# Another hand-written order of issue for a linear-attention and token-mixing kernel, with more wide matmul forms and two queues for the first loads

## The chip, the core and the metric

The kernel runs on one core of one Trainium2 chip. The time is device microseconds (us) of one execution. A core has five engines that run side by side and meet at semaphores: TensorE (PE in the profile, its weight loads PEld), VectorE (DVE), ScalarE (ACT), GpSimd (POOL) and SyncE (SP), which here issues transfers. Transfers themselves run on the core's 16 DMA engines.

## What is computed

For 8 batches of 8 heads, with 576 positions and a head size of 64, a linear attention with cosine weights, and then a token mixer over the joined heads:

```python
q_p = phi(q, cos_w, sin_w); k_p = phi(k, cos_w, sin_w)   # relu(x)*cos, relu(x)*sin
kv  = einsum('bhsf,bhsd->bhfd', k_p, v);  z = sum(k_p, axis=2)
num = einsum('bhsf,bhfd->bhsd', q_p, kv)
den = einsum('bhsf,bhf->bhs', q_p, z)[..., None] + 1e-06
x   = (num / den) with heads joined: 8 x 576 x 512
wq, wk = x @ w_q, x @ w_k                                 # 64 wide
mixed  = einsum('bst,btd->bsd', scale * (wq @ wk.T), x)
out    = maximum(mixed, 0) @ w_out                        # 8 x 576 x 512, fp32
```

The kernel never forms wq @ wk.T: it multiplies wk.T with x first.

## The kernel before, in words

**Work units.** A half batch is four heads of one batch (numbers 0 to 15, the H of the code; batch = H // 2). Its q, k and v come as two pieces a and b of 128 x 576 fp32 (0.295 MB each), into four raw buffers per tensor (`NRAW`), which are used in turn: half batch H's load waits until half batch H - 4's values have been read. The position is laid out as 64 partitions x 9, and two heads share the 128 partitions.

**The order.** Nothing is scheduled by a program at run time. `ORDER` (L24) is a string of words; the loop at L588 reads them one by one and emits each word's instructions. Every engine runs its own words in the order in which they stand, and waits by semaphores for what the other engines have to supply; a word that waits holds up all the later words of its engine. A word is a step, a number, `:` a PSUM bank (or pair of banks) and `@` an engine (A ScalarE, V VectorE, G GpSimd).

- **Loads and stores** (`load` L134, `LW` L564, `ST` L561): `LK3b` loads piece b of half batch 3's k, `LW` a weight matrix, `ST5` stores output tile 5 (of 36, each 128 x 512 fp32, 0.262 MB). All stand on SyncE's queue. A store waits for the copy `OE` of the same number, and what stands behind it in the queue waits too.
- **Tables at the start**: `TQ`, `TI`, `TK` on GpSimd (position numbers and an identity), `TV` and `TW` on ScalarE (their sines, with a table load ahead), `TP`, `T2`, `TZ` on VectorE (copies of a table, zeros).
- **Attention of a half batch**: `RK`, `RQ` (L216, L220: relu and cast of k and q), `CV` (L224: cast of v), `VS` (L227: v times cos and sin; on GpSimd two multiplications straight from the raw v, on VectorE one from the cast v). Then TensorE: `QT` or `QU` (transposes of q), `KV` or `KU` (k'v and the row sums of k), and two `N` (numerator and denominator). `QM` (VectorE) multiplies the transposed q with cos and sin on its way out of PSUM, `KE` takes k'v out, `EJ` and `RC` take the denominators and invert them, and two `X` (L340) make x. `XT` or `XR` transposes x, `XE` takes it out.
- **Mixer of a batch**: `WK`, `WQ` (products with the two small weights, `KW` and `QW` take them out), `KX` (wk.T x, taken out by `XK` into two halves of the partitions), `XA` and `XB` (copies of each half across to the other 64 partitions, `copy_across` L514), four `MX` with `ME` (product with wq, relu). Batches 4 and 5 are treated as a pair by another set of words (`WC`, `QC`, `WT`, `KC`, `KP`, `XP`, `MP`, `MM`). For two batches together follow nine `WO` (L547, product with w_out) and `OE` (L555, copy out into one of 16 buffers).

**Two forms of one step.** `KV` (L251) uses 36 matmuls of 64 rows x 64 columns of weights with 130 moving columns, one for each position group, pair of heads and row half; four of them fit on the array beside each other. `KU` (L278) uses 18 of 64 x 128 with 260 moving columns; half of what it computes (products across heads) is not used. `QT` (L263) uses 18 transposes of 64 rows, `QU` (L272) nine of 128 rows; `XR` (L370) 20, `XT` (L359) ten. After `KU`, `KE` takes out a result twice as long, and after `QU`, `QM` is two instructions.

Of the kernel before, what the change touches and what calls it, by code (L numbers as in the profile page):

```python
# [66 lines left out]
def kernel(  # L67
# [66 lines left out]
    def load(nm, H, part):  # L134
        b, h = divmod(H, 2)
        for r in (0, 1) if part is None else (part,):
            nc.sync.dma_start(raw[nm][H % NRAW][:, r, :], src[nm][b][:, 2 * h + r, :])
# [494 lines left out]
```

## Time and profile before

| what | value |
|---|---|
| time, median of 3 runs | 117.86 us (117.85 to 120.2) |
| time of the profiled execution | 117.42 us |
| its span, first to last instruction | 115.4 us |
| mean granted TensorE clock | 0.995 |
| matmuls | 2129 |
| transfers | 39.36 MB, 341 GB/s over the span |
| read, written | 29.62 MB, 9.44 MB |

Engines: PE is matmuls, PEld weight loads, and a busy share is of the span. The slices cut the span into 40 equal parts (2.9 us), with a digit for the busy share of each in tenths. The chain follows the work that ended last back from the last instruction, each piece released by the one ahead of it. In a row of the timeline or of the chain stand start, length, engine, line of the kernel, what it writes and reads, and how many; brackets give the idle time of the engine just before and what ended it. A matmul's row gives its shape as rows * columns of weights, then moving columns. The rows of a group give busy time and mean ns of one. SPq is the queue of SyncE, on which a row is the issue of a transfer, not the transfer.

### The profile page before, as it was taken

The page shows a single profiled execution, that of the slowest core. Times are in us where ns is not written, and L with a number is a line of the kernel's source. Part 1 is how long each engine was busy: PE and PEld are TensorE (multiplying, and loading weights), DVE is VectorE, ACT ScalarE, POOL GpSimd, SP SyncE. Part 2 cuts the span into 40 slices and gives each one's busy share as a digit, 9 for nine tenths or more (in the row PEclk, how much of TensorE's full clock was granted, in tenths as well). Part 3 has the DMA queues.
Part 4 walks back from the last instruction along what each step waited for, and adds up shares of the span by engine and source line. Part 5 has one row for each costly group of instructions (what it writes and reads, how often), then busy time and mean ns, then how long its engine had stood idle before and what let it go on. Part 6 is the DMA issues. An engine that isn't in the chain of part 4 may idle for free.

```text
span 115.4 us, 4951 instructions
## 1 busy us (share of the span) xinstructions
PE 95.5 (83%) x2129; PEld 63.3 (55%) x2129; DVE 83.0 (72%) x138; ACT 73.9 (64%) x124; POOL 72.7 (63%) x64
## 2 busy tenths in 40 slices
PE   0024976648999899999999999999999999999960
...
DMA  3999999999999999999999999999996450199994
GB/s 91 368 379 408 393 392 353 361 385 387 383 363 375 393 385 386 383 398 382 388 384 393 392 394 396 390 397 403 400 407 226 162 190 26 56 349 379 383 383 183
DMA packets 20660, 39.36 MB, mean 341 GB/s; under 512 B 3232, under 2 KB 3232, under 8 KB 20640
## 3 DMA queue, kind: packets, MB, share of 16 engines
...
q8 instruction: 16, 0.26, 0.9%
q14 instruction: 4, 0.03, 0.1%
HBM read 29.62 MB, written 9.44 MB: 339 GB/s over the span
## 4 chain that ended last, share of the span: by engine, by line
PE 64%; DMA 25%; ACT 4%; issue 1%; SPq 1%; POOL 1%; POOLq 0%
PE ps L552 29%; DMA vraw<-in_v_dram 15%; PE ps L319 7%; DMA kraw<-in_k_dram 5%; PE ps L258 5%; DMA qraw<-in_q_dram 5%; PE ps L535 3%; PE ps L276 3%; PE ps L380 2%; PE ps L416 2%; PE ps L403 2%; PE ps L506 2%; PE ps L441 2%; PE ps L367 2%; PE ps L269 1%
## 5 line engine op out<-in xcount | busy, mean ns | idle before, releaser
L233 POOL TENSOR_TENSOR v<-vraw,vtab 128x1152 bf16<-128x1152 f32 x20 | 42.1, 2128 | 3.0 <-PE ps L258 1.2
L552 PE MATMUL ps<-wow,mix 128*128 128x512 bf16 x144 | 34.7, 380 | 0.0
L344 DVE TENSOR_TENSOR x<-ps,rec 128x640 bf16<-128x640 f32 x32 | 24.9, 819 | 0.8
L208 ACT COPY o<-ps 128x512 f32<-128x512 f32 x26 | 15.1, 584 | 8.7 <-PE ps L552 8.7
L552 PEld LDWEIGHTS <-mix 128*128 128x128 bf16 x144 | 12.6, 98 | 14.1 <-issue 1.1
L319 PE MATMUL ps<-kvs,qm 64*128 64x65 bf16 x640 | 13.8, 193 | 1.1 <-ACT kvs L208 1.0
L204 POOL TENSOR_SCALAR rq<-qraw 128x1152 bf16<-128x1152 f32 (+1 forms) x10 | 10.5, 1050 | 6.4 <-DMA qraw<-in_q_dram 6.2
L526 ACT ACTIVATE mix<-ps 128x576 bf16<-128x576 f32 x20 | 12.3, 650 | 3.4 <-PE ps L535 3.0
L319 PEld LDWEIGHTS <-qm 64*128 64x128 bf16 x640 | 12.1, 96 | 3.4 <-issue 1.6
L208 ACT COPY xT<-ps 128x640 f32<-128x640 f32 (+1 forms) x15 | 10.1, 674 | 4.8 <-PE ps L380 2.9
L258 PE MATMUL ps<-v,rk 64*64 64x130 bf16 x468 | 10.6, 234 | 3.1 <-DVE v L236 1.4
L303 DVE TENSOR_TENSOR qm<-ps,qtab 128x2304 bf16<-128x2304 bf16 x9 | 12.2, 1352 | 1.0 <-PE ps L269 1.0
L204 POOL TENSOR_SCALAR rk<-kraw 128x1152 bf16<-128x1152 f32 (+1 forms) x10 | 10.0, 1002 | 4.1 <-DMA kraw<-in_k_dram 3.7
L212 DVE COPY o<-ps 128x512 f32<-128x512 f32 x10 | 6.9, 686 | 7.6 <-PE ps L552 5.2
L258 PEld LDWEIGHTS <-rk 64*64 64x64 bf16 x468 | 8.4, 114 | 5.9 <-issue 2.5
L269 PE MATMUL ps<-ident,rq 64*128 64x64 bf16 x162 | 4.1, 196 | 8.7 <-POOL rq L204 8.4
L208 ACT CAST kvs<-ps 128x260 bf16<-128x260 f32 (+1 forms) x12 | 5.2, 431 | 8.6 <-PE ps L258 7.1
L300 DVE TENSOR_TENSOR qm<-ps,qtab 128x1152 bf16<-128x1152 bf16 x14 | 9.7, 748 | 1.1 <-PE ps L276 1.1
L528 DVE TENSOR_SCALAR mix<-ps 128x576 bf16<-128x576 f32 x12 | 9.0, 753 | 2.1 <-PE ps L486 1.5
L202 ACT ACTIVATE rk<-kraw 128x1152 bf16<-128x1152 f32 (+1 forms) x8 | 8.8, 1103 | 1.6 <-DMA kraw<-in_k_dram 1.6
L236 DVE TENSOR_TENSOR v<-vb,ps 128x1152 bf16<-128x1152 bf16 (+1 forms) x8 | 8.3, 1042 | 1.6 <-POOL vb L210 1.3
L269 PEld LDWEIGHTS <-rq 64*128 64x128 bf16 x162 | 3.2, 98 | 10.0 <-POOL rq L204 9.3
...
## 6 DMA issues: line engine op xcount, KB each, us to landing
kraw<-in_k_dram SPq DMA_DIRECT2D x32, 288.0 KB, 5.9
vraw<-in_v_dram SPq DMA_DIRECT2D x32, 288.0 KB, 5.9
qraw<-in_q_dram SPq DMA_DIRECT2D x32, 288.0 KB, 5.9
...
```

The source lines that it names most:

```text
L202: A.activation(dst, s, AF.Relu)
L204: eng.tensor_scalar(dst, s, FMAX, 0.0, op0=ALU.min, op1=ALU.max)
L208: A.copy(dst, s)
L233: G.tensor_tensor(o[:, :, :, s].rearrange("p r c d -> p (r c) d"), v, vtab[:, 0:n * C, s, 0:1].to_broadcast([P, n * C, D]), op=ALU.mult)
L258: nc.tensor.matmul(kv_v[o, r, :], rk_b[H % NPREP][a, c, pr, :], v2_b[H % NV2][a, pr, c, :, 0:D + 1], start=(c == 0), stop=(c == C - 1))
L300: V.tensor_mul(qm_b[H % NQM][:, s, :, 0:C, :], q, qtab[:, s].unsqueeze(1).to_broadcast([P, 2, C, H2]))
L303: V.tensor_mul(qm_b[H % NQM][:, :, :, 0:C, :].rearrange("p s r c d -> p s r (c d)"), qt_view(at).unsqueeze(1).to_broadcast([P, 2, 2, S]), ...
L319: nc.tensor.matmul(nv[:, pr, u, :], qm_b[H % NQM][a, s, r, 2 * u:2 * u + 2, :], kv_b[H % NKV][a, r, pr if place["KV", H][1] else 0, s, 0:D ...
L344: V.tensor_tensor(x_b[b % NX][:, :, 4 * h:4 * h + 4, :].rearrange("p u (w r) d -> p r w u d", r=2)[:, r], num(place["N", g])[:, :, :, 0:D] ...
L526: A.activation(dst, s, AF.Relu, scale=scale_moe)
L528: V.tensor_scalar(dst, s, scale_moe, 0.0, op0=ALU.mult, op1=ALU.max)
L552: nc.tensor.matmul(o, mix_b[bp % 2][:, m, rt * P:(rt + 1) * P], wow[:, m, :], start=(m == 0), stop=(m == NDM - 1))
```

## The change

The string `ORDER` is replaced by another one. The work is the same; what differs:

- It begins with half batch 0 where the old one began with half batch 1. Three of the first six loads (`LQ0a`, `LV0b`, `LQ0b`) are issued by ScalarE, for which `load` gets an engine; the other loads and all stores stay on SyncE.
- Forms: `KU` for half batches 2, 3, 4, 7, 8, 9, 10, 12 (before 2, 8, 9), `QU` for 1, 2, 4, 5, 6, 7, 9, 10, 15 (before 0, 4, 6, 7, 8, 10, 11), `XT` for 0, 2, 3, 5, 7, 8 (before 1, 2, 5, 6, 9). 2129 matmuls become 2011.
- Engines: whole `VS` go from ten on GpSimd and four on VectorE to eight and six (and four halves on VectorE, as before), whole `CV` from three on GpSimd and one on ScalarE to six on GpSimd; `XE` from 15 on ScalarE and one on VectorE to 11 and five; `KW` all on ScalarE; some `KE`, `QW`, `XK`, `QC`, `KC`, `EJ`, `ME`, `MM`, `RK`, `RQ`, `CW` move singly.
- `copy_across` on ScalarE copies the 256 bf16 values as 128 fp32 words (8 of the 12 copies).
- Stores: `ST11`, `ST7`, `ST1`, `ST0`, `ST9`, `ST13`, `ST17`, `ST6` stand ahead of the last load, which is now `LK15a`; before it was eight others ahead of `LQ14a`.

The diff, with the order cut to the parts spoken of:

```diff
@@ ORDER @@
-TQ TI LK1b LV1a LQ1a TK RQ1a@G LV1b RK1b@G CV1a@A TV TW LQ1b CV1b@A TP0 TZ0@V T2 VS1b@V VS1a@V
-RQ1b@G LK1a QT1:0 RK1a@G LQ0b LQ0a LV0b LV0a LK0b CV0b@G CV0a@G LK0a LV2b LV2a LK2b LK2a QM1
-KV1:2 RQ0b@A KE1@A RQ0a@A LQ2a LQ2b LV3a LV3b LQ3b LW1 LK3b LQ3a RK0a@A LW0 LK3a RK0b@G LV4b LV4a
-VS0b@V LK4a LW2 LQ4b LQ4a CV2@G N3:2 RK2@G LV5a LK4b LQ5a LQ5b LW5 LV5b LW3 RQ2@G LW4 LK5a LK5b
-N2:0 EJ1@V RC1 VS0a@V QU0:4 QM0 KV0:6 KE0@A X3 N0:6 X2 N1:4 VS2@V LV6a LV6b CW1@G CV3@G EJ0@V
-XT1:0 XE1@A RC0 X1 KU2:2 X0 QT2:0 KE2@A XR0:6 XE0@A QM2 RQ3@G VS3@V CW0@G RK3@G WK0:6 N5:0 KW0@A
-KX0:6 XK0@A XB0@A QT3:2 QM3 N4:4 VS4@G KV3:6 EJ2@A RC2 X4 KE3@A XA0@A RK4@G WQ0:2 RQ5@G X5 N6:6
-QW0@A LQ7a LQ6a LQ6b LK6b LK6a LV7b N7:4 MX2:2 ME2@A EJ3@V RC3 CW5@G X7 MX1:0 RQ4@A CV5@G XT2:2
-X6 MX3:4 XR3:6 LV7a LK7b LQ7b LK7a XE2@A XE3@A ME1@V LQ8b QU4:2 QM4 LQ8a ME3@A MX0:0 ME0@A WK1:6
-KV4:4 KW1@V QT5:2 KX1:6 KE4@A LV8b LV8a QM5 WQ1:7 QW1@V N8:4 N9:2 CW2@A CW3@A EJ4@A VS5@V RC4
-XK1@A CW4@G X9 WO3:0 X8 WO1:1 OE1:0@A OE3:1@V RK5@G XB1@G KV5:6 XA1@A MX4:2 KE5@A LV9b LV9a MX6:4
-MX5:6 WO0:1 ME5@A VS6@G ME4@V ME6@V MX7:2 OE0:2@A N11:6 RQ6@A N10:4 ME7@V RK6@A XR4:0 WO5:2 WO2:3
...
-X14 QW2@A X15 XK2@V RK8@A XA2@A XB2@A XR7:4 QT9:0 VS9@V KU8:2 QM9 RQ10@G XE7@A MX8:6 KE8@A WK3:4
-N17:2 KW3@V ME8@A N16:0 EJ8@V RC8 MX11:4 KU9:6 X17 X16 ME11@A WQ3:4 KE9@A QW3@V MX10:2 ME10@A
...
-WC4:4 OE9:14@A XR10:0 LQ15a LV15b ST0 LQ15b LV14b LV14a ST8 LK12a LK12b X23 LK14a LK14b LV15a
-ST13 ST16 ST3 LK15b LK15a ST7 LQ14a ST5 ST12 ST15 RQ12@G VS12@G X22 XR11:6 QC4@V XE10@A QT13:2
...
-WO29:0 MX30:4 ME30@A WO30:1 WO31:4 OE30:13@A OE29:7@V WO33:5 OE31:8@A WO34:4 ST10 ST23 WO35:1
-ST21 ST19 ST22 ST1 ST26 ST25 ST18 OE33:3@A ST27 ST28 ST9 ST20 WO32:5 ST30 OE34:10@A ST31 ST29
-ST33 OE32:2@A ST34 OE35:1@V ST35 ST32
+LK0b LQ0a@A LV0a LV0b@A LK0a LQ0b@A TQ TI RQ0a@G TK TV RK0b@A TW CV0b@A CV0a@A RK0a@A LQ1a
+RQ0b@A LV1a LQ1b LV1b LK1a TP0 T2 LK1b LV2a LV2b LK2b LQ2b LQ2a LK2a LQ3b LQ3a LW0 LW1 LV3a LV3b
+RQ1b@G CV1b@G CV1a@A RQ1a@A VS0b@V LK3a LK3b LV4a VS0a@V LV4b LK4b LK4a TZ0@V QT0:0 KV0:2 KE0@A
+LQ4a QM0 LQ4b VS1a@V LQ5b LQ5a VS1b@V LW3 QU1:4 LW4 LV5a LV5b LW5 RK1a@G LW2 RK1b@A LK5b LK5a
+N1:2 VS2@G LV6b LV6a N0:0 EJ0@A QM1 RC0 X1 KV1:6 KE1@A N3:6 N2:4 RQ2@A CW1@G CW0@G CV3@G X0
+RK2@A RQ3@A EJ1@V XT0:0 RC1 X2 QU2:4 X3 XR1:6 KU2:2 QM2 QT3:4 KE2@A N4:2 XE0@A XE1@V N5:6 WK0:0
+QM3 EJ2@V RC2 VS3@V RK3@G KW0@A WQ0:4 KX0:5 XK0@A QW0@A XB0@A X5 KU3:0 CV4@G RK4@G KE3@A X4
+MX2:6 RQ4@G VS4@V MX3:4 RQ5@G XT2:2 N6:0 ME3@A N7:4 CV5@G CW5@G LQ7a LQ6a ME2@A RK5@G EJ3@V
+XE2@A XA0@A LQ6b LK6b LK6a LQ7b RC3 X7 KU4:6 MX0:2 ME0@A QU4:4 X6 XT3:0 KE4@A MX1:6 QU5:2 QM4
+XE3@A WK1:0 ME1@V QM5 CW4@A N8:4 KW1@A CW3@A CW2@A N9:6 KX1:0 WQ1:1 EJ4@V RC4 LQ8a X8 LV7a LV7b
+LK7b LK7a WO3:2 LV8a LV8b X9 VS5@V WO2:3 LQ8b LV9a LK8b LK8a LV9b VS6@G RQ6@G QW1@A OE3:0@A
+XK1@A XB1@A OE2:1@V WO0:2 OE0:2@V XA1@A MX7:0 RQ7@G MX4:6 ME4@A KV5:4 KE5@A MX6:2 ME6@V ME7@A
+LQ11a LK9b LQ9b LQ9a LV10b LK9a LV10a CV7@G WO1:6 OE1:3@A MX5:0 ME5@V N10:2 N11:4 EJ5@A RK7@G
...
+OE4:8@A ME10@V LK11b QT8:6 RK8@A XR6:2 XE6@V KU7:4 MX9:0 QM8 KE7@A ME9@A KU8:2 KE8@A N15:4 MX8:0
+ME8@A MX11:6 ME11@V VS9@G N14:2 RQ9@A EJ7@V WO11:6 OE11:9@A RC7 RK9@A WO12:0 X15 X14 LV13a LQ11b
+LQ12a LV13b QU9:6 N17:2 N16:4 OE12:10@V EJ8@A KU9:0 QM9 VS10@G KE9@A RC8 X17 XT7:6 N19:0 X16
+N18:2 EJ9@V RC9 XE7@A WK3:6 X19 X18 RK10@A KW3@A WQ3:4 CV11@G KX3:5 KU10:0 QW3@A RQ10@G VS11@V
...
+WO9:5 XP2@A QM12 MP19:2 MP21:6 MM19@V MP18:0 OE9:9@A MM21@V MM18@A WO16:4 MP16:0 MP23:2 KU12:6
+OE16:7@A KE12@A MM16@A MM23@V ST9 CV14@G RQ14@G MP22:2 KV13:4 LK15b ST13 ST17 ST6 LK15a ST2 ST5
...
+WO32:6 WO31:4 WO34:5 OE30:3@A OE29:2@V WO35:1 OE32:9@V OE34:14@V ST14 ST16 ST25 ST20 OE31:6@A
+WO33:0 ST8 ST3 ST19 ST30 ST29 OE35:12@A ST32 ST27 ST31 ST34 ST35 OE33:8@V ST33 WO28:1 OE28:15@A
+ST28
@@ -131,10 +132,10 @@
 
     src = {"k": srcs(k), "q": srcs(q), "v": srcs(v)}
 
-    def load(nm, H, part):
+    def load(nm, H, part, eng):
         b, h = divmod(H, 2)
         for r in (0, 1) if part is None else (part,):
-            nc.sync.dma_start(raw[nm][H % NRAW][:, r, :], src[nm][b][:, 2 * h + r, :])
+            (eng or nc.sync).dma_start(raw[nm][H % NRAW][:, r, :], src[nm][b][:, 2 * h + r, :])
 
     coef = math.pi / 2.0 / S
     ki = pool.tile([P, C, 2], I32, name="ki")
@@ -512,8 +513,11 @@
         cast(eng, kx_b[b % 2][:, 0, :], bank(place["KX", b])[:, 0:XC])
 
     def copy_across(b, t, eng):
-        cast(eng, kx_b[b % 2][H2 * (1 - t):H2 * (2 - t), 1, :],
-             kx_b[b % 2][H2 * t:H2 * t + H2, 0, :])
+        dst = kx_b[b % 2][H2 * (1 - t):H2 * (2 - t), 1, :]
+        s = kx_b[b % 2][H2 * t:H2 * t + H2, 0, :]
+        if eng is A:
+            dst, s = dst.bitcast(FP32), s.bitcast(FP32)
+        cast(eng, dst, s)
 
     def XA(b, ps, eng):
         copy_across(b, 0, eng)
@@ -593,7 +597,7 @@
         kind = word[:2] if word[:2] in steps or word[0] in "LRCVT" else word[0]
         i, ps = int(word[len(kind):] or 0), int(ps or 0)
         if kind in ("LK", "LQ", "LV"):
-            load(kind[1].lower(), i, part)
+            load(kind[1].lower(), i, part, ENG.get(eng))
         elif kind in halves:
             halves[kind](i, ps, ENG.get(eng), slice(0, 2) if part is None else
                          slice(part, part + 1))
```

More of the change, by code (lines that the diff above doesn't have):

```diff
@@ L49 @@
-ST13 ST16 ST3 LK15b LK15a ST7 LQ14a ST5 ST12 ST15 RQ12@G VS12@G X22 XR11:6 QC4@V XE10@A QT13:2
-WO14:4 ST11 XE11@V WC5:6 WO17:5 QM13 QC5@V QT12:2 WT2:6 KC2@V RK13@A VS13@G RK12@G OE14:15@A QM12
-OE17:8@A RQ15@A WO10:4 KP2:5 OE10:3@A KV13:2 XP2@A MP22:4 KE13@A MP20:6 MM22@A MM20@V MP16:0
-MM16@A KV12:2 MP23:4 KE12@V MP21:6 MM21@V MM23@A MP19:0 MM19@A N25:2 N24:4 MP18:6 MM18@A EJ12@V
-RC12 WO21:0 X25 WO26:1 X24 MP17:2 N27:6 OE21:2@A OE26:6@A N26:4 QT15:0 EJ13@A MM17@V WO25:2
-WO24:3 RC13 RK15@A RQ14@A X27 X26 OE24:13@A OE25:12@A VS15@G WO19:6 QM15 KV15:4 KE15@A ST14
@@ L55 @@
-XR13:2 OE19:1@V ST24 ST6 ST17 QT14:0 XE13@A N31:4 N30:6 RK14@G VS14@G EJ15@A WO18:2 WO22:3 QM14
-RC15 OE18:5@A X30 X31 OE22:4@A KV14:0 XR12:6 XR15:4 KE14@V XE12@A N29:0 N28:2 EJ14@V WK6:6 RC14
-X29 WQ6:7 KW6@A X28 QW6@A KX6:6 XE15@A XK6@A XA6@G WO23:0 XR14:6 MX24:4 OE23:10@V ME24@V XE14@A
-XB6@A WO20:2 WK7:3 MX25:4 MX27:6 KW7@V OE20:11@A ME27@A ME25@V MX26:0 WQ7:2 ME26@A KX7:3 WO28:0
-WO27:1 OE27:9@V XK7@A XA7@A QW7@A XB7@G MX28:2 MX29:4 MX31:6 OE28:15@A ME29@A ME28@V ME31@A
-WO29:0 MX30:4 ME30@A WO30:1 WO31:4 OE30:13@A OE29:7@V WO33:5 OE31:8@A WO34:4 ST10 ST23 WO35:1
@@ new lines @@
+LV15a ST0 LV14a LQ15b LQ15a KV11:2 LK14b QM10 QT11:0 ME15@A MX14:6 KE11@A N20:4 VS13@G RQ12@G
+N21:2 VS12@G QM11 ME14@A RK13@G RK12@G EJ10@V WO17:6 RC10 WO10:0 OE17:11@A X20 OE10:12@A N22:6
+X21 N23:4 EJ11@V RC11 X22 XR9:2 WO14:0 OE14:13@A XE9@A WO13:1 XR10:6 XE10@A RQ13@A X23 XR11:4
+OE13:14@V WC4:2 XE11@V WC5:4 WO15:6 QC4@V QC5@A WT2:4 QT13:2 QT12:0 OE15:15@A KC2@A KP2:4 QM13
+WO9:5 XP2@A QM12 MP19:2 MP21:6 MM19@V MP18:0 OE9:9@A MM21@V MM18@A WO16:4 MP16:0 MP23:2 KU12:6
+OE16:7@A KE12@A MM16@A MM23@V ST9 CV14@G RQ14@G MP22:2 KV13:4 LK15b ST13 ST17 ST6 LK15a ST2 ST5
```

22 lines of the change are left out of this document (13 added, 9 removed).

## The prediction, before any run

> **What bounds the kernel now.** I read the page's busy table and slices first, then the chain, then the timeline of the first 36 us, then the groups by line.
>
> ```profile
> PE 95.5 (83%) x2129; PEld 63.3 (55%) x2129; DVE 83.0 (72%) x138; ACT 73.9 (64%) x124; POOL 72.7 (63%) x64
> PE   0024976648999899999999999999999999999960
> DMA  3999999999999999999999999999996450199994
> GB/s 91 368 379 408 393 392 353 361 385 387 383 363 375 393 385 386 383 398 382 388 384 393 392 394 396 390 397 403 400 407 226 162 190 26 56 349 379 383 383 183
> ```
>
> A slice is 2.9 us. The DMA engines are full from slice 2 to slice 30, at about 0.38 MB per us; TensorE has holes until slice 11 and none after it. So there are two stages. Up to about 33 us the arrival of the inputs sets the pace. From there TensorE does, and the transfers have slack: they fall to 26 GB/s while TensorE stays full, and rise again when the last stores come. The chain says the same in time:
>
> ```profile
> 25.60 5.88 DMA qraw<-in_q_dram
> 31.65 1.16 POOL rq L204
> 32.85 0.44 PE ps L269 x18
> 37.24 0.49 issue
> 39.20 0.97 PE ps L552 x4
> 41.31 1.83 PE ps L552 x8
> 48.88 0.72 PE ps L258 x35
> 58.35 1.01 PE ps L284 x18
> 70.06 0.65 PE ps L258 x35
> 87.57 2.72 PE ps L552 x12
> 111.63 0.58 ACT o L208
> ```
>
> The columns are start, length and what. A transfer of q for half batch 5 lands, GpSimd does its relu (RQ5), the transposes QT5 follow, and then TensorE's steps run one after another until 111.6 us; after that come one output copy and one store. The first output step, WO3, is the mark between the two stages in both orders: in both it follows WQ1, and the steps ahead of it are the same work.
>
> ```profile
> 35.16 1.90 PE L552 MATMUL ps<-wow,mix 128*128 128x512 bf16 x8
> ```
>
> From WO3 to TensorE's end are 111.6 - 35.2 = 76.4 us. The profiled execution took 117.42 us with a span of 115.4, so 2.0 us lie around the span; the median of the runs is 117.86. The sum below is made against 117.42.
>
> **Part 1: the wide forms, after WO3.** Only forms change; every half batch still gets its steps. Eight KU for three and eight KV for thirteen take 90 matmuls out, nine QU for seven another 18, six XT for five 10: 2129 - 118 = 2011. What a form costs TensorE is read from the chain. Four WO matmuls with another shape behind them took 0.97 us, eight took 1.83, twelve 2.72: a WO takes 0.87, and a change of the matmul shape (128*128, 64*128, 64*64, 128*64) 0.1. KV took 0.65 with one such change behind it, so 0.56 by itself; KU (18 matmuls, 260 columns, two at a time) took 1.01. A KU in place of a KV thus costs 0.46 us and can save shape changes, because N, MX, XR and QT have its shape 64*128. Behind WO3 the new order has three more KU (7, 10, 12), as many QU and XT as before, and I count 54 shape changes against 59. 3 x 0.46 - 5 x 0.1 = **+0.9 us**, on the path, with nothing to hide it. Bounds: +0.4 (if the changes of shape saved are worth twice that) to +1.4 (if nothing).
>
> **Part 2: the start.** The new order begins with half batch 0 and waits more on ScalarE.
>
> ```profile
> 3.05 0.43 SPq L137 DMA_DIRECT2D kraw<-in_k_dram  x1
> 4.32 0.67 ACT L208 CAST vb<-vraw 128x576 bf16<-128x576 f32 x1 [2.30 <-DMA vraw<-in_v_dram]
> 6.47 1.15 ACT L182 ACTIVATE qtab<-wof 128x1152 bf16<-128x1152 int32 x1
> 7.81 0.66 PE L269 MATMUL ps<-ident,rq 64*128 64x64 bf16 x18 [7.81 <-POOL rq L204]
> 8.50 0.68 ACT L202 ACTIVATE rq<-qraw 128x576 bf16<-128x576 f32 x1 [0.33 <-DMA qraw<-in_q_dram]
> L167 ACT ACT_TABLE_LOAD x1 | 1.3, 1283 | 0.0
> qraw<-in_q_dram SPq DMA_DIRECT2D x32, 288.0 KB, 5.9
> ```
>
> The sixth transfer is issued at 3.05 us already, one per 0.47 us, while 0.295 MB need 0.78 us at 0.38 MB per us: issue is ahead of the data. Two queues therefore bring the six transfers at most the 0.4 us of one issue; I take 0. ScalarE now issues three of them (3 x 0.43) before its table load (1.28), which is free, since TV waits for TK, and TK now stands behind RQ0a on GpSimd: RQ0a starts with its data at about 4.3 (as the cast of v did), 0.67, TK 0.5, so TV at 5.5 and RK0b at 5.7. Then in ScalarE's order TW 1.1, two casts of v, RK0a and RQ0b at 0.67 each: RQ0b ends at about 10.0. QT0, which needs it, starts at 10.05 against 7.81 now: **2.2 us late**. KV0, KE0 and N0 wait behind it in turn. What hides this is the pace of the data:
>
> ```profile
> 24.50 1.15 POOL L204 TENSOR_SCALAR rk<-kraw 128x1152 bf16<-128x1152 f32 x1
> 25.70 0.72 PE L258 MATMUL ps<-v,rk 64*64 64x130 bf16 x36 [1.17 <-POOL rk L204]
> 30.09 1.15 POOL L204 TENSOR_SCALAR rk<-kraw 128x1152 bf16<-128x1152 f32 x1
> 31.65 1.15 POOL L204 TENSOR_SCALAR rq<-qraw 128x1152 bf16<-128x1152 f32 x1 [0.41 <-DMA qraw<-in_q_dram]
> ```
>
> Half batch 3's k is complete after 7.34 MB of loads in both orders, so RK3 again ends at 25.6 and KU3 starts there. Adding up TensorE's steps ahead of it (KV1 13.9, XT0 16.8, KU2 19.1, WK0 21.7, KX0 22.9) I find it ready at 23.6: the late start is used up with 2 us to spare, and KX0 and WQ0 lie ahead of KU3. Half batch 5's q is complete at 9.70 MB, now at 10.26, 0.56 / 0.38 = 1.5 us earlier: RQ5 runs from 30.15 to 31.3. Meanwhile VectorE, which has VS3 and VS4 now (1.27 each; VS4 was GpSimd's), goes VS3 25.4, X5, X4 26.9, VS4 28.2, EJ3, RC3, X7, X6 30.2; so KU4 28.2 to 29.3, QU4 29.7, XT3 30.3, QU5 31.3, and back to back WK1 0.68, N8 and N9 0.7, KX1 0.65, WQ1 0.6: WO3 at 34.55, **-0.6 us**. KU3's, KU4's, QU1's and QU2's greater length lies in these waits for data; without that cover it is 2 x 0.46 and 2 x 0.25. Bounds: -1.0 (the two queues bring their 0.4) to +2.2 (the late start is not absorbed).
>
> **Part 3: the other engines.** Busy times now, and what moves:
>
> ```profile
> L233 POOL TENSOR_TENSOR v<-vraw,vtab 128x1152 bf16<-128x1152 f32 x20 | 42.1, 2128 | 3.0 <-PE ps L258 1.2 <-DVE x L344 1.0 <-DMA vraw<-in_v_dram 0.7
> L236 DVE TENSOR_TENSOR v<-vb,ps 128x2304 bf16<-128x2304 bf16 x4 | 5.4, 1346 | 1.3 <-POOL vb L210 1.3
> L210 POOL TENSOR_SCALAR vb<-vraw 128x1152 bf16<-128x1152 f32 x3 | 3.5, 1151 | 1.7 <-DMA vraw<-in_v_dram 1.7
> L208 ACT COPY xT<-ps 128x640 f32<-128x640 f32 x10 | 6.9, 692 | 2.9 <-PE ps L380 2.9
> L212 DVE COPY xT<-ps 128x1280 bf16<-128x1280 bf16 x1 | 0.8, 811 | 0.0
> L208 ACT COPY kx<-kx 64x256 bf16<-64x256 bf16 x9 | 3.6, 403 | 0.2
> 35.00:60.00 25.00, 24.06 (x538) 16.48 (x530) 22.98 (x39) 17.83 (x29) 20.77 (x14) 1.00 1.04 387
> ```
>
> GpSimd loses two VS (2 x 4.26) and gets three casts of v (3 x 1.15), with small moves some 6 us less. VectorE gets two VS (2.7) and four XE (3.2), and gives three KW, a KE, an XK, a QW, a QC and a KC (2.9): some +3 us. ScalarE gives the XE and one table load; eight copies across halves as 128 fp32 words instead of 256 bf16 save something like 0.1 each: some 1.4 us less. None of this is on TensorE's path unless TensorE comes to wait. It does already a little: From WO3 on, 36 WO at 0.86, 9 KV 0.56, 22 N 0.31, 28 MX and MP 0.12, 9 XR 0.29, 5 QU 0.50, 5 QT 0.26, 3 XT 0.56, 2 KU 1.02, 4 each of WK, WQ and KX 0.59, 0.50 and 0.56, 2 WC 0.98, KP and WT 1.2 make 65.9 us (the shortest of each kind in the chain), and 59 shape changes 5.6: so 4.9 us of the 76.4 are small stops, such as the 0.49 in KV5, which waits for nothing that the profile shows. VectorE is the one to watch: 22.98 busy of 25 us from 35 to 60. For stops I take 0.1 less for the shorter copies, with bounds of -2.5 (half of them go) and +2.6 (VectorE sets the pace, below).
>
> **Part 4: stores.** Eight stores stand ahead of the last load in both orders, so this load lands at about the same time; ST9 asks for OE9, which I place at 79 us, about 1.6 us after its turn, behind which LK15b waits, but eight transfers in flight (5.9 us) cover that. Behind the last load the queue stood still in the old order; the new one has more stores that are ready:
>
> ```profile
> 81.60 30.97 SPq L562 DMA_DIRECT2D out_dram<-o  x28
> 95.00:100.00 5.00, 5.00 (x135) 3.40 (x128) 3.22 (x7) 3.00 (x6) 0.40 (x1) 1.00 0.09 32
> ```
>
> The last store is issued right after its copy now, so an earlier drain brings nothing: 0.
>
> **The sum:** 117.42 - 0.6 + 0.9 - 0.1 = **117.6 us**, 0.3 below the median shown: no change that 2% (2.4 us, about what a measurement of this kernel can tell from no change) would show.
>
> **The rivals.**
> (B) The small stops go. GpSimd's relief and the other order take half of the 4.9 us out, and the two queues bring their 0.4: 117.42 - 1.0 + 0.9 - 2.5 = 114.8. For it: ScalarE and GpSimd have less to do. Against: each stop is short, and VectorE has more.
> (C) Slower, the late start is carried: if TensorE isn't ready at 23.6 but later than 25.6, every further us is paid at WO3. With the whole 2.2: 117.42 + 2.2 + 0.9 = 120.5. For it: five ScalarE steps in a row stand ahead of QT0. Against: the 2 us to spare.
> (D) VectorE becomes the bound behind WO3. From RC4 to RC14, whose rows are
>
> ```profile
> 36.23 0.27 DVE L338 RECIPROCAL rec<-rec 128x20 f32<-128x20 f32 x1
> 96.36 0.28 DVE L338 RECIPROCAL rec<-rec 128x20 f32<-128x20 f32 x1
> ```
>
> it has 52.3 us of work by the groups' means against 50.1 now, done in 60.1 us; at the same ratio 62.7, +2.6: 117.42 - 0.6 + 2.6 = 119.4, part 1 hidden behind it.
> (E) What counts is the number of matmuls. By the page's 95.5 us for 2129, 118 fewer are worth 5.3 us: 112.1. Against: KV's 36 took 0.65, KU's 18 took 1.01.
> [...]
> (F) The two queues and the fp32 copies do nothing and ST9's stop does reach the last k (KV15): 1.6 more, 119.2.
>
> **How the numbers follow.** Forecast 0.50 (its own range 116.2 to 119.0), B 0.22, C 0.13, D 0.09, E 0.03, F 0.03. Faster by over 2% (under 115.5): most of B, E, a little of the forecast's edge, 0.24. Slower (over 120.2): most of C, a third of D, 0.14. Within: 0.62. The range 114.5 to 120.8 goes a little past B's value and C's, and leaves out the outer parts of B and C, and E.
>
> **What would show it.** Right: QT0 at about 10 us; KU3 at 25 to 26 and released by RK3; WO3 at 34 to 35; KU 1.0 us each with KV at 0.65; 77 us from WO3 to the last matmul; no transfers waiting at the end. Wrong: WO3 later than 36 (C), VectorE over 94% busy in a stretch of 20 us while TensorE has holes (D), WO3 to the end under 75 us (B).

## The result, and the profile after

| | before | after |
|---|---|---|
| median of 20 runs each, us | 118.12 (116.81 to 120.2) | 119.25 (118.32 to 120.47) |
| ratio, with its 95% interval | | 1.0117 [1.0084, 1.0151] |
| span of the profiled execution, us | 115.4 | 116.9 |

The change makes the kernel slower by 1.2%, some 1.4 us (the medians differ by 1.1); the forecast was 0.15% above the profiled time of before and 0.3 us below the median shown with it, that is, no change. Ratios here leave out runs more than 1.5% above a kernel's fastest one, so they can differ from the ratio of the medians (most in experiment 4). One kernel varies by 1 to 2 us either way from run to run. The profiled execution of before (117.42 us) lies below its kernel's median, that of after (119.83 us) above, so this pair lies further apart than usual.

The page of the changed kernel: span, busy times, three rows of slices (2.92 us each) and the two queues over which the engines' own instructions come (packets, MB, share).

```profile
span 116.9 us, 4706 instructions
...
PE 96.0 (82%) x1997; PEld 65.0 (56%) x2011; DVE 86.8 (74%) x139; ACT 71.9 (62%) x127; POOL 66.8 (57%) x61
...
PE   0004977967999899998999979999998999999940
...
DMA  3999999999999999999999999995993198980992
GB/s 87 393 399 389 393 384 336 393 390 389 385 393 392 391 387 386 391 390 396 387 391 395 403 394 397 368 390 208 296 373 147 53 379 331 344 333 8 353 377 81
...
q8 instruction: 15, 0.25, 0.9%
q14 instruction: 5, 0.04, 0.1%
```

The two stages are still there: transfers full to slice 27, then TensorE. (14 matmul records are missing in this trace; 2011 weight loads are there.) Behind slice 11 TensorE has an 8, a 7 and an 8 (slices 19, 24 and 31) where before had nines. New is the 8 GB/s of slice 37 (105 to 108 us), where the stores stand, and the last two queue rows, which matter below.

The timeline's rows of the marks (start, length, matmuls of QT0, KU3, WO3), then pieces of the chain (start, length, what):

```profile
10.26 0.67 PE L270 MATMUL ps<-ident,rq 64*128 64x64 bf16 x18 [10.26 <-ACT rq L203]
...
24.94 1.19 PE L285 MATMUL ps<-v,rk 64*128 64x260 bf16 x18 [0.91 <-POOL rk L205]
...
34.44 1.89 PE L556 MATMUL ps<-wow,mix 128*128 128x512 bf16 x7
```

```profile
51.21 1.01 PE ps L285 x18
...
69.41 0.61 issue
70.02 0.38 PE ps L556
...
106.18 6.16 PE ps L556 x28
...
112.36 0.59 ACT o L209
```

The start came as forecast, and so did KU's 1.01 us. TensorE ends at 112.34 (106.18 + 6.16), 0.7 us later than before although it reached WO3 0.7 us earlier. The account, profile against profile; "stops" are all gaps over 0.09 us behind WO3 in which TensorE neither multiplies nor loads weights, from the trace's records; "work" is the rest:

| | before | after | difference | forecast |
|---|---|---|---|---|
| to WO3 | 35.16 | 34.44 | -0.7 | -0.6 |
| WO3 to last matmul, work | 75.45 | 76.24 | +0.8 | +0.9 |
| the same, stops | 0.99 | 1.66 | +0.7 | -0.1 |
| last store's issue to its last packet | 1.76 | 2.45 | +0.7 | 0 |

The row of the stops is the least certain. 0.12 of the 1.66 us, ahead of WO9, is a matmul without a record: the traces of experiments 3 and 13, which have all of them, show no gap there. And stops differ between executions of one order: the traces of experiments 9 and 14, in which TensorE's instructions are those of before, have 2.7 and 1.9 us of them.

**The end.** The transfers from 110 us to the end of the span, before and then after, 0.14 and 0.17 us to a number:

```profile
DMA  9999999999998999999999999989700000000000
GB/s 364 394 394 349 395 379 425 349 380 349 394 440 334 410 349 394 349 379 455 349 394 334 394 380 379 440 334 410 258 0 0 0 0 0 0 0 0 0 0 0
...
q1 hardware_dynamic: 818, 1.48, 73.3%
```

```profile
GB/s 392 380 356 404 392 416 297 416 427 380 356 380 416 380 368 392 380 368 392 380 356 356 345 356 416 356 60 12 24 24 36 0 0 0 0 0 0 0 0 0
...
q1 hardware_dynamic: 951, 1.72, 66.5%
q14 instruction: 1, 0.01, 0.5%
```

Before, all transfers stop together. After, a rest goes on at some 24 GB/s: by the records, 8 packets of the last store (2 KB, 84 ns each) run one behind the other from 114.78 to 115.43, alone. 8 are one engine's share of a store's 128 packets, and 24 GB/s about a sixteenth of the 385 or so ahead of them, so 15 engines have stopped and one goes on (the records don't name it). And in this window, and not in that of before, there is one packet of the instruction queue q14, 8 KB, from 114.23 to 114.78: the 8 packets begin when it ends.

**A stop in the middle.** The 0.61 us of "issue" stand ahead of the last of WO10's four matmuls. A window on the transfers just ahead of it:

```profile
q1 hardware_dynamic: 223, 0.45, 99.5%
q8 instruction: 1, 0.02, 5.6%
```

Among the loads runs one packet of the other instruction queue, 16 KB, by the records from 67.56 to 68.64; TensorE goes on at 70.02, 1.39 us after its end. This gave a theory: **TensorE runs out of instructions.** The trace of before has 16 such packets for 4258 matmuls and weight loads, that of after 15 for 4022: 266 and 268 to a packet. I took a packet for a block of 256 instructions; that length is shown by the places of the stops, below. Its rival was that the order lost time to waits for data of VectorE, ScalarE and GpSimd.

### The profile page after: what moved, and what is told of

It reads as the page before. It is cut to its first block, busy times and chain, and to the rows that moved or that the text cites. A ratio compares the mean times of both kernels' runs of the same rounds, so it can differ in the third digit from the quotient of the medians.

```text
span 116.9 us, 4706 instructions
## 1 busy us (share of the span) xinstructions
PE 96.0 (82%) x1997; PEld 65.0 (56%) x2011; DVE 86.8 (74%) x139; ACT 71.9 (62%) x127; POOL 66.8 (57%) x61
## 4 chain that ended last, share of the span: by engine, by line
PE 57%; DMA 20%; DVE 11%; ACT 4%; issue 2%; POOL 1%; ACTq 0%; SPq 0%; POOLq 0%; DVEq 0%
PE ps L556 23%; DMA vraw<-in_v_dram 9%; DMA qraw<-in_q_dram 6%; PE ps L285 6%; PE ps L320 5%; DMA kraw<-in_k_dram 5%; DVE v L237 3%; PE ps L539 3%; PE ps L277 3%; DVE x L345 3%; PE ps L381 3%; PE ps L404 2%; PE ps L259 2%; PE ps L507 2%; PE ps L417 2%
## 5 line engine op out<-in xcount | busy, mean ns | idle before, releaser
L234 POOL TENSOR_TENSOR v<-vraw,vtab 128x1152 bf16<-128x1152 f32 x16 | 33.7, 2129 | 5.8 <-PE ps L320 1.8
L301 DVE TENSOR_TENSOR qm<-ps,qtab 128x1152 bf16<-128x1152 bf16 x18 | 12.7, 749 | 1.0 <-ACT o L209 0.5
L237 DVE TENSOR_TENSOR v<-vb,ps 128x2304 bf16<-128x2304 bf16 (+1 forms) x10 | 10.9, 1110 | 3.1 <-ACT vb L209 1.8
L532 DVE TENSOR_SCALAR mix<-ps 128x576 bf16<-128x576 f32 x14 | 10.5, 753 | 3.7 <-PE ps L539 2.8
L304 DVE TENSOR_TENSOR qm<-ps,qtab 128x2304 bf16<-128x2304 bf16 x7 | 9.4, 1352 | 2.2 <-PE ps L270 1.9
L285 PE MATMUL ps<-v,rk 64*128 64x260 bf16 x144 | 9.6, 271 | 1.6 <-POOL rk L205 0.9
L211 POOL TENSOR_SCALAR vb<-vraw 128x1152 bf16<-128x1152 f32 (+1 forms) x7 | 7.6, 1083 | 4.8 <-DMA vraw<-in_v_dram 4.7
L209 ACT CAST kvs<-ps 128x520 bf16<-128x520 f32 (+1 forms) x13 | 6.4, 494 | 5.7 <-PE ps L285 3.0
L211 POOL TENSOR_SCALAR kx<-kx 64x256 bf16<-64x256 bf16 x4 | 1.6, 399 | 14.0 <-ACT kx L209 13.8
L285 PEld LDWEIGHTS <-rk 64*128 64x128 bf16 x144 | 7.1, 93 | 3.0 <-POOL rk L205 1.4
```

The costliest lines, as they stand in the source:

```text
L209: A.copy(dst, s)
L234: G.tensor_tensor(o[:, :, :, s].rearrange("p r c d -> p (r c) d"), v, vtab[:, 0:n * C, s, 0:1].to_broadcast([P, n * C, D]), op=ALU.mult)
L237: V.tensor_mul(o.rearrange("p r c s (h e) -> p (r c) s h e", e=2), vb_b[H % NPREP][:, part].rearrange("p r c (h e) -> p (r c) h e", e=2).u ...
L285: nc.tensor.matmul(o[:, r, :], rk_b[H % NPREP][a, c, :, :], v2_b[H % NV2][a, :, c, :, 0:D + 1], start=(c == 0), stop=(c == C - 1))
L301: V.tensor_mul(qm_b[H % NQM][:, s, :, 0:C, :], q, qtab[:, s].unsqueeze(1).to_broadcast([P, 2, C, H2]))
L532: V.tensor_scalar(dst, s, scale_moe, 0.0, op0=ALU.mult, op1=ALU.max)
```

## The experiments

All were timed in 5 rounds against the kernel before on the same chip: 1 to 4, 5 to 12, 13 to 15 and 16 to 18 on one chip each. What the change does is undone in parts first (1 to 4), then the instruction blocks are shifted (5 to 7, 10, 11), then the end is tested (8, 9, 13, 16 to 18); 12 and 14 put parts of the change into the kernel before, and 15 joins the two orders once more. "Theory" and "rival" are those of the text recorded for each experiment.

**1 and 2, the two halves of the order.** The new order up to WO3 with the old one behind it, and the reverse; steps already done are left out of the second part.

```diff
 # 1: new order ... LV7b LK7b LK7a
-WO3:2 LV8a LV8b X9 ...
+LQ8b LV8b LV8a QW1@V VS5@V XK1@A X9 WO3:0 WO1:1 ... (old order to its end)
```

> The new order's words up to WO3, then the old order's words (less those already done), so the new start with the old middle and end. My account of the 1.4 us: the start gains 0.7 at WO3 (34.45 against 35.16 in the profiles) and the rest loses about 2.2. By it this kernel is 0.7 us faster than before, ratio 0.994, WO3 at 34.5. Rival (what the start gains is given back later, because data or stores set the end anyway): ratio 1.000 within 0.003. Second rival (the late first transposes are what costs): 1.005 or more.

Measured 119.41 us, 1.0136 [1.0081, 1.0190]. WO3 came at 34.45, yet the last matmul at 113.43: stops of 0.84 (KV5), 0.85 (N15), 0.71 (XR11) and 0.42 us (N29) took the gain and more; work from WO3 on was 75.40, as before. By its size this is the second rival, but not by its reason, as WO3 came as early as expected.

> The old order's words up to WO3, then the new order's. By my account 2.2 us slower than before, ratio 1.018, WO3 at 35.2. Rival (the start is given back): 1.012, as the changed kernel. Second rival (the start costs): 1.005 or less.

Measured 123.69 us, 1.0454 [1.0387, 1.0522], far above both. A stop of 2.26 us ahead of WO3 itself (released by VectorE's X), and two of 0.57 and 0.59 us. Right behind the first one the granted clock was 0.5 from 38.05 to 41.47 us, and twelve WO matmuls took 4.45 us there, against 2.72 in the kernel before: 1.7 us of the time is the clock. So neither half has a price of its own: what is done ahead decides where the other half stops.

**3, the stores.** ST27, ready first, ahead of ST30, for which the queue stood.

```diff
-ST30 ST29 OE35:12@A ST32 ST27
+ST27 ST30 ST29 OE35:12@A ST32
```

> The new order with one word moved: ST27 stands ahead of ST30 in SyncE's queue instead of behind ST30, ST29 and ST32. In the new profile OE27 is ready at 105.3 and ST27 is issued at 109.2, behind ST30, which waits for OE30 until 107.4, while the DMA engines move 80 GB/s. My account: the ten stores from 107.4 on are more than the engines can move until the last copy (113.0), and the last store lands 0.75 us later after its issue than it did before; with nine it is 0.6 to 0.7 us faster than the new order, ratio to before 1.006. Rival (TensorE and the last copy set the end, the longer last landing is chance): as the new order, 1.012.

Measured 119.06 us, 1.0098 [1.0056, 1.0140], an interval that holds both values; the trace decides for the rival. The late engine was there again, behind a q14 packet from 114.13 to 114.88, and last issue to last packet was 2.41 us.

**4, the three wide forms undone.**

```diff
-KU7:4 ... KU10:0 ... KU12:6
+KV7:4 ... KV10:0 ... KV12:6
```

> The new order with KV in place of KU for half batches 7, 10 and 12, nothing else. My sum: three times 0.46 us of streaming back, five changes of matmul shape more: 0.9 us faster than the new order, ratio to before 1.004, TensorE's last matmul at 111.4 instead of 112.3. Rival (TensorE's added streaming lies in waits for the other engines): as the new order, 1.012.

Measured 121.86 us, 1.0151 [1.0084, 1.0219] for the faster of its runs (two of six): not cheaper, as my sum had it; whether dearer than the change (1.0117), these two don't say. The chain of its profiled execution (123.06 us) has

```profile
67.83 2.34 issue
...
100.42 0.47 issue
```

and a stop of 0.95 us at KV10. A KV is 72 instructions where KU is 36. Right behind the stop of 2.34 us the granted clock was 0.5 again, from 69.94 to 73.36, so the work from WO3 on, 77.1 us, doesn't price the forms. Without the 1.7 us that the clock cost in experiment 2 it is 75.4 (an estimate), 0.8 less than after, about what part 1 has for the forms.

**5, 6, 7: the blocks shifted.** One-column matmuls of a zeroed tile, two instructions each, run in the first 3 us, where TensorE has nothing to do. They move every later instruction by 224, 256 (one whole block) and 280 places.

```diff
     def WU(i, ps, eng):
-        pass
+        V.memset(zt, 0.0)
+        for j in range(i):
+            a, o = (slice(H2 * r, H2 * r + H2) for r in (j % 2, j // 2 % 2))
+            nc.tensor.matmul(bank(ps + j % 2)[o, 0:1], zt[a, 0:H2], zt[a, H2:H2 + 1],
+                             start=True, stop=True)
 # ORDER begins with WU112:4, WU128:4 or WU140:4
```

> The changed kernel with 112 one-column matmuls of a zeroed tile on TensorE ahead of everything, where TensorE stands idle; they write a PSUM bank that is overwritten later. Each is two instructions, so every later instruction of TensorE stands 224 places further on in the blocks of 256 in which its instructions are fetched. Theory (TensorE's program is fetched too slowly where many small matmuls stand close): at this shift the shortest time between a block's start and the place 70 instructions ahead of its end is 4.3 us, against 3.35 us without it (at 69 us, where the 0.61 us stop stands), so that stop goes and no new one comes: ratio to before about 1.006, 0.6 us less than the change. Rival (the 0.61 us stop is a wait for data or a property of that matmul): the stop stays at the same matmul, ratio 1.012.

> The same with 128 matmuls, 256 instructions: one whole block, so every place within a block is as in the change. Both theories: ratio about 1.012, the 0.61 us stop ahead of the same matmul. If the idle matmuls by themselves changed the time (TensorE's clock at the start), it would show here.

> The same with 140 matmuls, 280 instructions: 24 places beyond one block. Theory: the shortest stretch is now 1.8 to 2.3 us (at 67 us, ahead of N20 to N23), while a fetch needs some 3.6 us to be usable; a stop of about 1.6 us there instead of 0.61, so 1 us more than the change: ratio about 1.021. Rival (stop not from the fetch): 1.012, the same stop of 0.61 us.

Measured 1.0120 [1.0085, 1.0155], 1.0072 [1.0041, 1.0102] and 1.0217 [1.0158, 1.0276]. With 140 the stop is now 1.18 us at N21, with another of 0.77 at KU10 (its chain has both),

```profile
63.64 0.77 issue
...
68.88 1.18 issue
```

and the kernel is 1.7 us slower than with 128 (120.87 against 119.18): the theory. With 128 a stop stands ahead of the same matmul of WO10 as forecast, but of 0.27 us, and one of 0.35 us stands one block earlier. With 112 the stop at WO10 is gone as expected, but no time was gained: in all three a wait for data of 0.4 us at WO5 came in (13, 16 and 17, without idle matmuls, have it too) and WO3 was 0.1 to 0.3 us later. The expectation of 1.006 failed.

The proof is the place of the stops. The next fences give for several kernels the time up to a stop with TensorE's busy time and the number of its matmuls and weight loads so far (first two groups); the first fence is the kernel before (its 0.49 us at KV5), then experiments 9 (0.25, 0.86, 0.76 us), 10 (1.20 us) and 12 (0.60, 1.26 us).

```profile
0.00:37.30 37.30, 22.25 (x606) 17.33 (x607) 25.85 (x46) 18.64 (x33) 25.04 (x36) 1.00 1.00 357
```

```profile
0.00:36.95 36.95, 22.21 (x606) 17.33 (x607) 26.17 (x47) 19.22 (x39) 24.99 (x36) 1.00 1.00 359
0.00:54.90 54.90, 39.36 (x990) 28.93 (x990) 42.18 (x75) 32.23 (x58) 40.06 (x44) 1.00 1.02 369
0.00:60.65 60.65, 44.25 (x1118) 32.97 (x1118) 47.12 (x82) 36.56 (x65) 45.27 (x48) 1.00 1.02 371
```

```profile
0.00:62.90 62.90, 48.19 (x1246) 35.76 (x1246) 47.89 (x83) 36.73 (x61) 46.84 (x49) 0.95 1.02 369
```

```profile
0.00:55.65 55.65, 40.77 (x990) 30.18 (x990) 42.82 (x75) 32.39 (x53) 40.07 (x44) 1.00 1.01 365
0.00:75.10 75.10, 59.31 (x1374) 43.16 (x1374) 58.71 (x102) 47.48 (x77) 56.31 (x54) 1.00 1.01 366
```

Add the two: 1213, 1980, 2236, 2492 and 2748. They lie 256 apart (1213 is 1212 and one), whatever the step is called: 606 + 607 in two kernels, 990 + 990 in two. In all, 30 stops of 0.2 us and more in 15 of the 20 traces stand within three instructions of such a place, and 29 of them ended 1.26 to 1.54 us after a 16 KB packet of q8 had ended (experiment 12's second at 76.33, its packet at 75.02; experiment 10's at 64.03, its packet at 62.64). The thirtieth, 0.44 us at N11 in experiment 15, is a wait for data. Counted on from 1212 in steps of 256, 16 such places lie in the kernel before (188 to 4028) and 15 in the changed one, as many as the packets of each. In the kernel before the packets began 2.3 to 3.8 us after TensorE had passed one of these places as long as the transfers were full (13 packets) and 0.7 to 1.6 us after it later, ended ahead of the next place, and took 0.9 to 1.1 us among full loads. That a packet begins only then is not shown: in the trace of after, the first twelve began 1.8 to 4.0 us after their places, the thirteenth 0.7 us ahead of its own, and the last two 1.3 and 0.5 us behind theirs. 3.0 + 1.05 + 1.4 makes 5.5 us a block (an estimate from the times of the kernel before and the 1.26 to 1.54 us). In experiment 9, TensorE went on at 55.72 and stood again at 60.61: 256 instructions in 4.9 us, and then 0.76 us without.

**10 and 11, shifts chosen to avoid the stops.** 84 idle matmuls ahead of the kernel before, 12 ahead of experiment 1's.

> The kernel before with 84 idle one-column matmuls (168 instructions) ahead of everything on TensorE. Theory of the fetch: at this shift no stretch between 30 and 92 us is shorter than 3.6 us (2.7 and 2.8 us at 84 and 72 us without it), so the stop of 0.49 us ahead of KV5 goes; with the 0.4 us that the idle matmuls cost the changed kernel by themselves elsewhere, ratio 0.996 to 1.000. Rival (KV5 waits for its data): the stop of 0.49 us stays at KV5, ratio 1.000 to 1.004.

> The first experiment again (the new order up to WO3, the old one behind it; ratio 1.0136, with stops of 0.84, 0.85, 0.71 and 0.42 us) with 12 idle matmuls, 24 instructions, ahead of everything on TensorE. Theory of the fetch: at this shift the shortest stretches behind WO3 are 3.3 us and more (2.65 us at 51 us without it); the stops at KV5, N15 and XR11 shrink from 2.4 us in sum to 0.5 to 1 us and the ratio to 0.998 to 1.003. Rival (the start's gain is lost to waits for data of VectorE and ScalarE): the stops stay at the same matmuls, ratio 1.0136.

Measured 1.0136 [1.0075, 1.0198] and 1.0078 [1.0034, 1.0122]; both expectations failed in size. In 10 the stop at KV5 went, but one of 1.20 us came at N18, and the profiled execution had a granted clock of 0.5 from 23.7 to 30.5 us and WO3 at 37.2; why the clock fell is open. In 11 the stops at N15, XR11 and N29 went as expected; the 0.76 us at KV5 stayed, so that one is a wait for data (it isn't at a block's end either). In 10 a stretch that I had called safe held a stop, because I had reckoned a fetch, and the 3.6 us that the expectation of 7 gives it (my estimate), from the wrong place: a block is entered some 60 counted instructions earlier than I took it, at the places above.

**12, the wide forms alone.** KV7, KV10 and KV12 of the kernel before made KU.

> The kernel before with KV7, KV10 and KV12 in the wide form and nothing else of the change. By the sum of the prediction (three times 0.46 less the shape changes 0.1 to 0.3): TensorE streams 1.0 to 1.3 us longer between WO3 and its last matmul, 76.5 us instead of 75.45 once the stops are taken off; ratio 1.009 if the stops stay as they are. Theory of the fetch: the three save 36 instructions each, so the stops move; between 0.5 us less and 1 us more of them. Rival (the wide form is no dearer among other work): streaming 75.5 us, ratio 1.000.

Measured 120.50 us, 1.0224 [1.0177, 1.0271]. Work from WO3 on was 75.92, only 0.47 more than before: the forms themselves cost half of what I expected, perhaps since a KU next to N, MX or XR saves more shape changes. But the stops were 3.01 us, 0.60 and 1.26 of it at block ends (0.99, 1.9 and 2.7 in the traces of before, 14 and 9), and the last store was late too. Three forms that cost half a microsecond cost 2.6 in this order.

**8, one queue for the first six transfers.**

```diff
-LK0b LQ0a@A LV0a LV0b@A LK0a LQ0b@A
+LK0b LQ0a LV0a LV0b LK0a LQ0b
```

> The changed kernel with the first six transfers all on SP's queue, so that ScalarE issues three instructions less. Theory of the tail (a fetch of 8 KB of ScalarE's own instructions, started 1.9 us after its instruction 190 or 191, occupies one DMA engine at 114.2 to 114.8 and makes the last store's share of that engine 0.7 us late): with 188 instructions ahead of the end it starts only after the last store, span less last issue goes from 3.9 to 3.1 us, and the ratio to 1.005 if the start is not later; if QT0 moves from 10.26 to 10.6 the gain is less by as much. Rival (the late engine has another cause): the tail stays 3.9 us, ratio 1.011 to 1.014.

Measured 119.19 us, 1.0080 [1.0026, 1.0134], between the two. The end is the theory's: in its trace the q14 packet came after the last store (116.44), and last issue to last packet was 1.67 us. WO3's first weight load came at 34.7 us (not at 34.2, as the expectation of 16 has it), and at 34.2 to 35.0 in six traces of the new start with two queues: no sign that two queues help.

**9, six tiny copies on ScalarE in the kernel before.** They make the late engine in a kernel that doesn't have it.

```diff
+        for j in range(i):
+            cast(A, zt[:, j + 1:j + 2], zt[:, 0:1])    # zt: a zeroed tile
 # ORDER begins with WU6
```

> The kernel before with six one-column copies of a zeroed tile on ScalarE where it waits for its first data. Nothing else changes. Theory of the tail: ScalarE passes its instruction 190 at its last copy (111.6 us) and not after the last store, so a fetch of 8 KB of its instructions runs at about 113.4 to 113.8 us on one DMA engine, in the last store; that engine's share ends after the others' and the span less the last issue goes from 3.1 to 3.5 to 3.9 us: ratio 1.003 to 1.007. Rival (the late engine of the change has another cause): 3.1 us and 1.000, all engines end together.

Measured 118.81 us, 1.0058 [1.0016, 1.0099]: the theory, though the profiled execution also has 2.7 us of stops. The transfers of its last 6.6 us (0.165 us to a number) show the tail of one engine and the packet:

```profile
GB/s 397 397 385 397 360 335 410 385 372 360 397 397 385 385 397 385 397 373 348 360 385 385 373 372 422 248 0 25 25 25 25 0 0 0 0 0 0 0 0 0
...
q14 instruction: 1, 0.01, 0.5%
```

**13, ten tiny copies on ScalarE in the changed kernel,** which bring the same fetch forward.

```diff
-LK0b LQ0a@A LV0a LV0b@A LK0a LQ0b@A TQ
+LK0b LQ0a@A LV0a LV0b@A LK0a LQ0b@A WU10 TQ    # ten copies as in 9
```

> The changed kernel with ten one-column copies of a zeroed tile on ScalarE, behind its three transfers and ahead of its first table. ScalarE passes its instruction 190 five copies earlier, at about 106 us, so the fetch of its instructions runs at about 108 us and no longer in the last store. Theory of the tail: the span less the last issue goes from 3.9 to 3.1 to 3.3 us, the ratio from 1.0117 to 1.005 to 1.007. Rival (any fetch late in the kernel costs the same because the transfers stand full from 103 us on): the end stays 3.7 to 3.9 us, ratio 1.010 to 1.013.

Measured 118.28 against 118.64 us, 0.9949 [0.9910, 0.9989], lower than the theory's 1.005 to 1.007. The packet ran at 104.26 to 104.73, the stores' standstill followed, and the engines ended together (110 us to the end, 0.135 us to a number):

```profile
GB/s 394 364 410 319 425 349 425 379 349 394 379 425 319 410 394 364 394 364 410 334 410 379 364 304 410 379 364 425 198 15 0 0 0 0 0 0 0 0 0 0
```

**14, the copies across alone,** in the kernel before.

> The kernel before with only the change's copies on ScalarE taken as half as many fp32 values. The prediction's step: about 0.1 us at most, ratio 1.000. Rival (ScalarE's shorter copies release KX's readers sooner and TensorE's data stops of 0.1 to 0.2 us with them): 0.997.

Measured 0.9868 [0.9788, 0.9948], from few runs; by the medians 0.994 (117.94 against 118.64). That is below both values, and the trace doesn't say why: a copy took 0.30 us instead of 0.40 (groups of after and before), and the work from WO3 on was 75.1 us, but the stops were 1.9. Experiment 17 asks again.

**15, a later joint.** The new order on one queue to MX5's copy, then the old one, with 12 idle matmuls and 8 tiny copies at the start.

> The changed kernel's order, on one queue, up to the copy behind MX5; from N10 and N11 on the old order; 12 idle matmuls on TensorE and 8 one-column copies on ScalarE at the start, so that the blocks of instructions fall as in the 11th experiment and ScalarE's late fetch comes near 109 us. Theory (the start's gain is real and only given back behind WO3 by the new order, the stops and the late fetch): WO3 at 34.2 us, no stop of 0.76 us at KV5, streaming 75.0 to 75.5 us from WO3, last matmul at 110.3 to 110.9 us against 111.6 before; ratio 0.990 to 0.998. Rival (an earlier TensorE only runs into the stores, which fill the transfers from 103 us on): the last packet stays at 114 us or later, ratio 0.999 to 1.005.

(In this mixture output tile 1 is overwritten in its buffer by tile 10 before it is stored; no work is left out.) Measured 119.94 against 118.64 us, 1.0117 [1.0069, 1.0165]: it fell out as neither. The stop at KV5 was gone, but waits for data of 0.44 (N11), 0.81 (KV7) and 0.51 us (QU8) and a fetch of 0.79 us (KX3) came; last matmul at 113.76. The start's gain was carried over by neither of two joints (1 and 15).

**16, 17, 18, on one chip:** one queue and the ten copies; the ten copies with bf16 copies across; the change itself.

> The changed kernel with all first transfers on SP's queue and the ten copies on ScalarE: the start of the eighth experiment (WO3 at 34.2 us) and the end of the thirteenth (span less last issue 3.1 us). Theory: 0 to 0.3 us below the thirteenth experiment, ratio 0.992 to 0.996. Rival (two queues are worth something once the end is mended): above it, 0.997 to 1.000.

> The thirteenth experiment with the copies across as in the kernel before, in bf16 on ScalarE too. By the prediction's step (0.1 us at most): ratio 0.995 to 0.996, as the thirteenth. Rival (the shorter copies are worth the 0.5% or more that the fourteenth experiment showed): 1.000 or more.

> The change itself, in the same call as the two above, for a comparison on one chip. Theory (the late fetch costs 0.7 us, stops that fall differently from run to run the rest): 0.7 to 1 us above the other two, ratio 1.002 to 1.008. Rival (this chip favours the new order, the ten copies do little): within 0.3 us of them, 0.995 to 0.998.

| | median, us | ratio |
|---|---|---|
| 18, the change | 119.16 | 1.0101 [1.0060, 1.0141] |
| 17, with ten copies, bf16 across | 118.32 | 1.0011 [0.9968, 1.0054] |
| 16, with ten copies, one queue | 118.65 | 1.0015 [0.9971, 1.0060] |

With ten copies of one column, and one more difference each, the change is 0.5 (16) to 0.8 us (17) faster, and no difference from the kernel before is left that these intervals show. All three ratios lie above their expectations: on this chip the new order seems to stand higher than on experiment 13's. Experiment 13's 0.9949 is the lowest of the new order; 16 and 17 show no gain over the kernel before, so I call it level. Two queues are worth nothing that shows. For the fp32 copies the runs disagree: 17, without them, came out on its rival's side and 0.6% above 13, and 14 was below 1, but on another chip; 16, with them and beside 17, has 17's ratio. Whether they bring more than the 0.1 us forecast is open.

**The end in all kernels,** last issue to last packet in us, and the fetch that lies in the last full stretch of stores (in the old order from about 103 us on, in the new one behind the standstill at 105 to 108, which in experiment 2 is at 112 to 114):

| kernels | fetch | us |
|---|---|---|
| before, 8, 13, 14, 16, 17, 2 | none | 1.67 to 1.76 |
| after, 3, 5, 6, 7, 18, 4 | ScalarE's (q14), 1.6 to 2.1 us after its last copy began | 2.37 to 2.51 |
| 9 | the same, at 115.0 | 2.54 |
| 1, 11, 15 | q14 at 110 to 113 (1 and 15 also q8, at 104.8 and 103.6) | 2.37 to 2.66 |
| 10, 12 | TensorE's (q8), at 103.6 and 105.4 | 2.71, 2.61 |

ScalarE has 194 instructions in the trace of after and 188 in that of before; in after the fetch began at 114.23, 1.87 us after the 190th and 191st (112.36 and 112.37), in before at 117.08, 1.77 us after the last of the 188. Three of the six are the transfers it issues now.

## Why the prediction was wrong

- **Part 1, +0.9: right in size.** The work between WO3 and the last matmul grew by 0.8; it is 75.1 to 75.5 us in three traces of the old order (before, 9, 14) and 76.1 to 76.5 in five of the new one (after, 3, 13, 17, 18). Its parts are off: the three KU came to 0.47 in experiment 12, not 3 x 0.46; the remaining 0.4 belongs to the order and no run isolates it.
- **Part 2, -0.6: right.** QT0 at 10.26 (10.05), KU3 at 24.94 (25.6), released by RK3, WO3 at 34.44 (34.55). WO3 comes at 34.2 to 35.0 in six traces of the new start and at 34.8 to 35.5 in four of the old (before, 9, 12, 14), so its gain holds beyond this pair, with scatter. The late start was absorbed by the pace of the data, and two queues brought nothing (experiment 8), as taken.
- **Part 3, -0.1: off by +0.8 in this pair of executions;** that it is off in general isn't shown. Its reckoning is wrong: of the "4.9 us of the 76.4" that it took for small stops, the records of before show 0.99; the rest lies within the steps, of which the sum took "the shortest of each kind". So rival B had little to gain.
  I had the key in hand, "such as the 0.49 in KV5, which waits for nothing that the profile shows", and took the small stops for something that shorter copies ease. The copies did get 0.1 us shorter each; what that is worth is open (14, 17).
  Stops at block ends were 0.49 and became 0.61, the others (0.1 to 0.3 us each: MX6, N14, WO17, KP2, WO9, N26) grew from 0.50 to 1.05. For the first kind the experiments show the cause, but not that the change has more of it: in executions with unshifted blocks they sum to 0.5, 2.4 and 1.8 us in the old order (before, 9, 14) and to 0.6, 0.3, 0, 0 and 0.6 in the new one (after, 3, 13, 17, 18). Experiments 7 and 12, with 1.9 us of them each, show what they can cost: 7 is 1.7 us slower than 6, and 12 is 2.6 us slower than before.
  The second kind are waits for data, each too small for a run of its own. Two of them are the order's: the 0.2 us at KP2 and the 0.3 at N26 stand in all 12 traces that end with the new order and in none of the 8 that end with the old one.
- **Part 4, 0: failed,** by +0.7. This is the step that failed, a term put at nothing. "The last store is issued right after its copy now, so an earlier drain brings nothing: 0" is true of the issue (0.64 us after the last matmul in both) and overlooked what shares the DMA engines with the last store: a fetch of ScalarE's instructions, 8 KB, which made one engine 0.7 us late. Nor was there an earlier drain: no store was issued from 102.9 to 107.4 us, and from there to the end the transfers were full, so that the sign "no transfers waiting at the end" did not come. Experiments 9 and 16 to 18 show this one from both sides: put into the old kernel it costs 0.6% [0.2, 1.0], and moved away in the new one it gives 0.5 to 0.8 us.
- **The rivals.** C (late start carried) and D (VectorE the bound) named places that the trace clears: KU3 was ready, and TensorE's small waits for VectorE sum to tenths. D's sign did just appear, with VectorE 94.6% busy from 46 to 66 us, but TensorE's stops there are 0.13 us. E's rule, that the number of matmuls counts, has a true core in another place: not as time of each, but as instructions to be fetched; fewer of them in another place came with longer stops (experiment 12), and putting matmuls back too (experiment 4).

So in this pair the change's 0.7 us of start went to slightly dearer work (0.8), and 0.7 us at stops and 0.7 us at the end make it slower. The end, from six instructions more on ScalarE, is shown to be the change's: without it no loss is left that 16 and 17 show. Of the stops, the 0.5 us at KP2 and N26 are its order's; for the rest that is not shown.
